# Moving the logarithm parts and their matrix passes within the woven order of a gated-linear-attention and squared-ReLU kernel

## The chip, the cores and the metric

The kernel runs on one core of one Trainium2 chip. The metric is the device time of one execution in microseconds, lower is better; the figure to start from is the median of eight runs. TensorE does the matrix products and the transposes, ScalarE (ACT) the logarithms, exponentials and many copies, VectorE (DVE) the elementwise work, SyncE (SP) issues all transfers between memory and the core.

## The reference

The first half is a recurrence over 768 time steps for 4 batches of 8 heads of 48 dimensions; the second half is a feed-forward layer with a squared ReLU on the 3072 rows that come out.

```python
def _attn_ref(q, k, v, alpha):
    B, H, S, D = q.shape                       # 4, 8, 768, 48
    state = np.zeros((B, H, D, D), dtype=np.float32)
    for t in range(S):
        state = alpha[:, :, t, :, None] * state + np.einsum('bhd,bhde->bhde', k[:, :, t], v[:, :, t])
        y[:, :, t] = np.einsum('bhd,bhde->bhe', q[:, :, t], state)

x = y.transpose(0, 2, 1, 3).reshape(B * S, H * D)     # 3072 x 384
h = np.maximum(x @ w_in, 0.0)                         # w_in 384 x 2048
out = (h * h) @ w_out                                 # w_out 2048 x 384
```

The kernel computes the recurrence in chunks: inside a chunk of 128 steps the running products of alpha are the exponentials of running sums of log(alpha). With b the running product, q is multiplied by b and k by 1/b, and the recurrence in a chunk becomes matrix products with a causal mask.

## The kernel before, in words

**Blocks, pairs and groups.** A block is one chunk of 128 steps of one batch, with all eight heads: 24 blocks, numbered `n`, four to a chunk position. Two blocks make a pair, four a group (`GB = 4`). The feed-forward layer works on one group of 512 rows at a time, six groups in all. While the layer works on group g, the attention of group g+1 is woven into its instructions.

**The attention of a block** is a row of small steps, named by functions: `ln` takes the logarithm of the block's alpha in place (ScalarE). `sp` splits it into two parts, `hi` rounded to the type fp32r and `lo` the rest (VectorE, lines 258 and 259). `cs` forms the running sums on TensorE: a triangular matrix times `hi`, then times `lo`, two passes that add up in one PSUM bank (lines 270 and 271). `eb` and `ei` are the exponentials of the sums and of their negatives (ScalarE, lines 278 and 282). `mq` and `mk` multiply q and k by them (VectorE, line 286). `bl` and `br` send the last row of b out to memory and back in another layout (SyncE). `turn` transposes q and k of both blocks (TensorE, line 535), `kc` and `qc` copy them out (ScalarE). `ga` and `gb` hold the scores, the masked copy, the chunk's state and the outputs `y`: bursts of 64 to 160 short matrix products on tiles of 48 or 64 rows (lines 400, 424, 450), with the mask, the sums and the next state on VectorE (lines 434, 461, 469, 470), and at the end of `gb` the copies of y into xT (ScalarE, line 558). The split exists from block 8 on (`SPLIT = 2 * GB`); the blocks before it multiply the unsplit logarithm.

**Buffers.** `hi` shares two buffers with the b of `eb` (tag "b"), `lo` two with the inverse of `ei` (tag "inv"). The sums of `cs`, the transposes, the scores and y all draw on one pool of four PSUM banks (`ps_att`); a bank is free again for a later tile, in program order, once the last reader of the tile in it is issued, and the first writer of the later tile waits for that reader. The product of a group's layer uses the other four banks.

**The layer from group 1 on** has two stages. First 38 us of `ffn_in_pair` (line 679) with no attention beside it. Its last steps are VectorE and ScalarE work on the hidden values (lines 692, 697, 698, 699) and one sum (line 590). Then 28 *units* of `ffn_product` (line 750), each eight matmul records of 128x192: four units to each of seven products, "1 5 6 7 2 4 3". After every unit of 5, 6 and 7 one sum on VectorE (line 590) prepares an operand of a later product.

**The order.** Nothing reorders this kernel: each engine's instructions run in the order in which the program lists them. The list is made by `weave`. A table, `PLAN`, gives each step a due time in units; a pair that starts at `t` has its step due at `t + at`. `weave` runs through the units and, ahead of unit u, issues every step whose due time is at most u, in order of due time, and those with equal times in order of the pairs. A digit behind a step's name says which block of the pair it is for. A `cs` step of block n also issues the load of block n+2's alpha, behind it in SyncE's queue; `ga`, `gb` and `turn` issue loads of k, v and q.

The pairs of split blocks and their starts: in group 1 blocks 8, 10 and 12 at t = 0, 7 and 14; in groups 2 and 3 blocks 14 and 18 at t = 0 and blocks 16 and 20 at t = 13.5; in group 4 block 22 at t = 0. Eight pairs in all. In group 0, whose layer is not of this form (units of `ffn_in` and `ffn_out`), blocks 4 and 6 are planned with due times stretched by 2.35, and the third pair there only closes block 6.

Of the kernel before, what the change touches and what calls it, by code (L numbers as in the profile page):

```python
# [24 lines left out]
def kernel(  # L25
# [224 lines left out]
    SPLIT = 2 * GB  # L250
# [564 lines left out]
    for word in first.split():  # L815
# [5 lines left out]


    PLAN = (
        (0, "ln0"),
        (0.5, "ln1 sp0"),
        (1.0, "sp1"),
        (2.0, "cs0 eb0 ei0"),
        (3.0, "cs1 eb1 ei1"),
        (3.5, "mk0"),
        (4.0, "bl0"),  # L830
        (4.5, "mq0 mk1 bl1"),
# [3 lines left out]
        (9.5, "ga"),  # L835
        (10.5, "gb"),
    )

    def attention(pairs, scale):


        out = []
        for t, n0, after, *last in pairs:
            for at, fs in PLAN:
                for f in fs.split():
                    w = t + at * scale
                    if f in ("ga", "gb"):
                        given = n0 - 2 if after else None, None if last or n0 >= NBLK else n0
                        out.append((w, {"ga": ga, "gb": gb}[f], given))
                    if last:  # L850
                        continue
                    if f == "ga" and n0 + 3 < NBLK:
                        out.append((w, load, (n0 + 3, "k")))
                    elif f == "gb":
                        for m, x in ((n0 + 2, "v"), (n0 + 3, "v"), (n0 + 4, "k")):
                            if m < NBLK:
                                out.append((w, load, (m, x)))
                    elif f == "turn":
                        if n0 < NBLK:
                            out.append((w, turn, (n0,)))  # L860
                            for m in range(n0 + 2, min(n0 + 4, NBLK)):
                                out.append((w, load, (m, "q")))
                    elif f != "ga" and n0 < NBLK:
                        n = n0 + int(f[-1])
                        out.append((w, steps[f[:-1]], (n,)))
                        if f[:-1] == "cs" and n + 2 < NBLK:
                            out.append((w, load, (n + 2, "a")))
        return sorted(out, key=lambda x: x[0])
# [18 lines left out]
    events += [(0, load, (GB + 1,)), (1.0, load, (GB + 2, "k"))]  # L887
    events += [(47 + 2 * r, sum_w_in, (r,)) for r in range(NR2 - 1)]
    events += attention([(0, GB, False), (18.0, GB + 2, True), (27.5, GB + 4, True, True)], 2.35)
    events += [(53, sum_x, (1,)), (54, sum_w_in, (NR2 - 1,))]  # L890
    weave(units, sorted(events, key=lambda x: x[0]))
    for g in range(1, NG):

        for j in range(NJ // 2 + 1):
            for i, step in enumerate("ABacCDd"):
                if j - step.islower() in range(NJ // 2):
                    ffn_in_pair(g, j - step.islower(), step)
                if g == 1 and j < NJ // 2 and i in (1, 4):
                    sum_w_out(2 * j + i // 4)
        events = []  # L900
        if g + 1 < NG:
            n = GB * (g + 1) + 2
            pairs = [(0, n, True), (13.5, n + 2, True)]
            if g == 1:
                pairs = [(0, n - 2, False), (7.0, n, True), (14.0, n + 2, True)]
            events = attention(pairs, 1) + [(NU - 3, sum_x, (g + 1,))]
        weave([(1, ffn_product, (g, *divmod(u, NR2))) for u in range(NU)], events)
# [30 lines left out]
```

## Time and profile before

| | |
|---|---|
| median of 8 runs | 568.5 us (568.05 to 571.26) |
| the profiled execution | 568.46 us, of which the span of the trace is 566.4 us |
| TensorE busy | 552.5 us, 98% of the span |
| weight loads | 470.1 us, 83% (they overlap the products) |
| VectorE / ScalarE busy | 339.9 us (60%) / 223.7 us (39%) |
| `cs` passes in the split blocks | 32: 16 on line 270, 16 on line 271 |
| `hi` / `lo` | 352 to 363 ns / 557 to 561 ns, 16 of each |

Matmul ends are modelled by the profile, so a busy TensorE is not TensorE at its peak. Where it loses time is read better from the distance between the starts of two neighbouring products than from the busy share. The stages lie as follows: group 1's `ffn_in_pair` ends at about 168.6 us and its units run to 225; then 38 us of `ffn_in_pair` and some 50 us of units for each of groups 2 (units 263 to 315), 3 (353 to 404) and 4 (442 to 488), and group 5 without attention to the end.

### The profile page before, as it was taken

Reading aid. Unit: us, or ns where it says so; the run is one execution under the profiler, and the core shown is the slowest. Engines: PE = TensorE matmul, PEld = TensorE weight load, DVE = VectorE, ACT = ScalarE, POOL = GpSimd, SP = SyncE. Lnnn points to the kernel's source line nnn. Section 1 sums busy time; section 2 is a strip of 40 time slices with the busy share of each in tenths; the row PEclk is TensorE's granted clock in tenths of the full one; section 3 lists DMA queues with packets and bytes.
Section 4 is the critical chain, followed back from the end, with each engine's and each line's share of the span. In section 5 each row is a group of like instructions: output and inputs, shape, how many; then the busy total and the mean of one; then the engine's idle time right before and its main releaser. Section 6 shows DMA issues by size and latency. Waiting matters only on the chain.

```text
span 566.4 us, 12584 instructions
## 1 busy us (share of the span) xinstructions
PE 552.5 (98%) x5306; PEld 470.1 (83%) x5306; DVE 339.9 (60%) x687; ACT 223.7 (39%) x533; POOL 5.9 (1%) x26
## 2 busy tenths in 40 slices
PE   8889999999999999999899999999999999999997
PEld 5754455668888999888899988999988999988996
DVE  4988688685875854566572566572466651466430
ACT  4469865442334353234243333432333340333100
POOL 2010000000000000000000000000000000000000
PEclk9999999999999999999999999999999999999999
DMA  9978577401003655000333200333300000100001
GB/s 164 253 175 219 144 163 238 114 1 57 1 1 56 114 97 104 30 1 17 55 72 77 65 2 0 57 72 58 86 0 1 0 3 1 57 0 1 1 0 57
DMA packets 117087, 37.04 MB, mean 65 GB/s; under 512 B 108820, under 2 KB 111912, under 8 KB 117032
## 3 DMA queue, kind: packets, MB, share of 16 engines
q1 hardware_dynamic: 117032, 36.25, 28.6%
q8 instruction: 42, 0.69, 0.5%
q14 instruction: 13, 0.11, 0.1%
HBM read 31.49 MB, written 4.75 MB: 64 GB/s over the span
## 4 chain that ended last, share of the span: by engine, by line
PE 62%; DVE 1%; ACT 1%; issue 1%
PE o L750 28%; PE h L679 27%; PE y L400 3%; PE sckv L424 1%; PE T L535 1%; PE sckv L450 1%; PE cs L271 1%; DVE lo L259 0%; ACT hid L698 0%; PE cs L270 0%; DVE hi L258 0%; DVE hid L692 0%; ACT hid L697 0%; DVE osb L784 0%; ACT qs L543 0%
## 5 line engine op out<-in xcount | busy, mean ns | idle before, releaser
L679 PE MATMUL h<-xT,w_in 128*128 128x256 f32 x480 | 124.0, 379 | 0.0
L679 PEld LDWEIGHTS h<-xT,w_in 128*128 128x128 f32 x480 | 91.1, 190 | 12.4
L750 PE MATMUL o<-w_out,hid 128*128 128x192 f32 x480 | 82.4, 326 | 0.0
L750 PEld LDWEIGHTS o<-w_out,hid 128*128 128x128 f32 x480 | 78.9, 190 | 0.4
L558 ACT COPY xT<-y 32x256 f32<-32x256 f32 (+2 forms) x132 | 46.2, 364 | 64.1 <-PE y L400 60.3
L692 DVE TENSOR_TENSOR hid<-h,u 128x256 f32<-128x256 f32 x120 | 50.8, 424 | 28.9 <-PE h L679 24.3
L697 ACT ACTIVATE hid<-hid 128x256 f32<-128x256 f32 x40 | 16.7, 417 | 114.6 <-DVE hid L692 114.6
L692 DVE TENSOR_TENSOR u<-h,u 128x256 f32<-128x256 f32 x80 | 33.9, 423 | 34.8 <-PE h L679 22.4
L679 PE MATMUL h<-s3x,ws 128*128 128x256 f32 x160 | 47.6, 379 | 0.0
L641 PE MATMUL h<-xT,w_in 128*128 128x512 f32 (+1 forms) x108 | 43.5, 550 | 3.3 <-ACT xT L558 1.8
L434 DVE COPY_PREDICATED am<-halves_mask,sckv 128x256 f32<-128x256 uint32 x40 | 15.6, 443 | 48.7 <-PE sckv L450 48.7
L716 PE MATMUL o<-w_out,hid 128*128 128x384 f32 x128 | 42.8, 490 | 0.0
L750 PE MATMUL o<-t,s 128*128 128x192 f32 x240 | 41.8, 327 | 0.0
L679 PE MATMUL h<-s3x,w_in 128*128 128x256 f32 x160 | 41.1, 379 | 0.0
L641 PEld LDWEIGHTS h<-xT,w_in 128*128 128x128 f32 x108 | 20.0, 190 | 23.4 <-issue 16.5
L750 PEld LDWEIGHTS o<-t,s 128*128 128x128 f32 x240 | 39.3, 190 | 0.2
L716 PEld LDWEIGHTS o<-w_out,hid 128*128 128x128 f32 x128 | 23.9, 190 | 16.2 <-issue 0.2
L679 PEld LDWEIGHTS h<-s3x,ws 128*128 128x128 f32 x160 | 30.4, 190 | 4.1
L679 PEld LDWEIGHTS h<-s3x,w_in 128*128 128x128 f32 x160 | 30.4, 190 | 4.1
L750 PE MATMUL o<-t,hid 128*128 128x192 f32 x160 | 28.1, 330 | 0.0
L784 DVE TENSOR_TENSOR osb<-o,us 128x384 f32<-128x384 f32 x10 | 5.6, 557 | 37.0 <-PE o L750 37.0
L699 DVE SCALAR_TENSOR_TENSOR hid<-hid 128x512 f32<-128x512 f32 x40 | 27.3, 682 | 0.0
(127 smaller groups left out, 767.9 us busy)
## 6 DMA issues: line engine op xcount, KB each, us to landing
raw<-in_moe_w_in_dram SPq DMA_DIRECT2D x8, 768.0 KB
raw<-in_moe_w_out_dram SPq DMA_DIRECT2D x8, 768.0 KB, 5.6
v_in<-in_v_dram SPq DMA_DIRECT2D x24, 192.0 KB, 3.8
out_dram<-osb SPq DMA_DIRECT2D x24, 192.0 KB, 2.1
k_in<-in_k_dram SPq DMA_DIRECT2D x23, 192.0 KB, 4.4
a_in<-in_alpha_dram SPq DMA_DIRECT2D x22, 192.0 KB, 3.6
q_in<-in_q_dram SPq DMA_DIRECT2D x22, 192.0 KB, 3.7
last<-row SPq DMA_DIRECT2D x40, 0.8 KB, 3.3
```

Source lines behind the costliest of these rows:

```text
L271: nc.tensor.matmul(out=out, lhsT=causal_r, rhs=lo, start=False, stop=True)
L400: ins = nc.tensor.matmul(out=ys[e][64 * half : 64 * half + D + G * e, m % 2, p // 2, t], lhsT=lhsT, rhs=rhs, start=(half, e) not in seen, ...
L424: nc.tensor.matmul(out=ps[e][HALF[h], 0, p, :], lhsT=ks[rows, p, HALF[h]], rhs=qs[rows, p, HALF[h]], start=True, stop=True, skip_group_che ...
L434: nc.vector.copy_predicated(out=am_h(n)[:, e, n % 2], data=ps[e][:, 0], mask=halves_mask.bitcast(U32).unsqueeze(1).to_broadcast([128, NP, ...
L558: copy(out=x[to : to + m, kk, t : t + 2], in_=blk[n]["y"][e][r : r + m, :, p // 2],)
L641: nc.tensor.matmul(out=ps, lhsT=w[:, kk, c0 : c0 + 128], rhs=xT[g][:, kk, cols], start=(kk == 0), stop=(kk == KM - 1),)
L679: nc.tensor.matmul(out=ps, lhsT=a, rhs=b, start=(step.isupper() and i == 0), stop=(i == len(pairs) - 1), skip_group_check=True,)
L692: nc.vector.tensor_tensor(out=o, in0=ps, in1=z, op=ALU.add)
L697: nc.scalar.activation(out=h1[:, HT : 2 * HT], in_=h1[:, HT : 2 * HT], func=AF.Relu)
L699: nc.vector.scalar_tensor_tensor(out=h2, in0=h2, scalar=0.0, in1=h2, op0=ALU.max, op1=ALU.mult)
L716: nc.tensor.matmul(out=acc[t][:, 0:DM], lhsT=hid[i][:, j, t * C : (t + 1) * C], rhs=w_out[i][:, j, :], start=(i == 0 and j == 0), stop=(i ...
L750: nc.tensor.matmul(out=acc[k][:, t, :], lhsT=lhs[:, j, t * C : (t + 1) * C], rhs=rhs[:, j, :], start=(first and r + j + t == 0), stop=(r = ...
```

## The change

`PLAN` gets new due times, and a second table, `EARLY`, keeps the old ones for blocks below 8, where there is no split.

```diff
     PLAN = (
-        (0, "ln0"),
-        (0.5, "ln1 sp0"),
-        (1.0, "sp1"),
-        (2.0, "cs0 eb0 ei0"),
-        (3.0, "cs1 eb1 ei1"),
+        (-1.0, "ln0"),
+        (-0.5, "ln1 sp0"),
+        (0.0, "sp1"),
+        (2.5, "cs0 cs1 eb0 ei0"),
+        (3.0, "eb1 ei1"),
         (3.5, "mk0"),
...
     )
+    EARLY = (
+        (0, "ln0"),
+        (0.5, "ln1"),
+        (2.0, "cs0 eb0 ei0"),
+        (3.0, "cs1 eb1 ei1"),
+    ) + tuple(x for x in PLAN if x[0] > 3)
...
-            for at, fs in PLAN:
+            for at, fs in EARLY if n0 < SPLIT else PLAN:
```

The logarithms of both blocks and their splits are due one unit sooner. The two passes of the second block come straight behind the two of the first: the first block's move half a unit later and the second's half a unit sooner. The exponentials of the first block move with its passes; those of the second keep their time. The loads of alpha that hang on `cs` move with them.

## The prediction

> **What bounds the kernel now.** The page first: TensorE is the busy engine all along, and its clock stays full.
>
> ```profile
> PE   8889999999999999999899999999999999999997
> DVE  4988688685875854566572566572466651466430
> PEclk9999999999999999999999999999999999999999
> ```
>
> TensorE is near nine tenths everywhere, VectorE at half, no slice below full clock. So only what holds TensorE up is worth anything, and a step moved on another engine matters only through TensorE. The table of waits names who holds it up near the change:
>
> ```profile
> PEld cs L271 <- DVE lo L259: 2.3, 6, 0.4
> PEld cs L270 <- DVE hi L258: 1.3, 4, 0.3
> PEld y L400 <- issue: 5.3, 13, 1.6
> ```
>
> Columns: total us, times, the longest. Weight loads of the logarithm passes wait 10 times, 3.6 us in all, for the parts hi and lo. Sixteen blocks have such passes, so not all wait. The timeline at the start of group 2's units:
>
> ```profile
> 263.10 2.76 PE L750 MATMUL o<-w_out,hid 128*128 128x192 f32 x16
> ...
> 265.86 0.56 DVE L259 TENSOR_TENSOR lo<-a_in,hi 128x384 fp32r<-128x384 f32 x1
> 265.88 0.19 PEld L270 LDWEIGHTS cs<-hi,causal_r 128*128 128x128 f32 x1 [0.32 <-DVE hi L258]
> ...
> 266.47 0.19 PEld L271 LDWEIGHTS cs<-lo,causal_r 128*128 128x128 f32 x1 [0.41 <-DVE lo L259]
> ...
> 266.73 0.56 DVE L259 TENSOR_TENSOR lo<-a_in,hi 128x384 fp32r<-128x384 f32 x1
> 266.75 1.46 PE L750 MATMUL o<-w_out,hid 128*128 128x192 f32 x8
> ...
> 268.05 0.19 PEld L271 LDWEIGHTS cs<-lo,causal_r 128*128 128x128 f32 x1
> ...
> 268.40 1.46 PE L750 MATMUL o<-w_out,hid 128*128 128x192 f32 x8
> ```
>
> Columns: start, duration, engine. Eight products take 1.46 us of which the last one's own 0.33 us overlaps what follows, so they step by (1.46 - 0.33)/7 = 0.162 us and a unit is 1.30 us. The last product of unit 1 starts at 263.10 + 2.76 - 0.33 = 265.53, the first of unit 2 at 266.75: 1.22 us for block 14's two passes. For block 15's two passes the same distance is 268.40 - (266.75 + 1.46 - 0.33) = 0.52 us, without a wait. The difference, 0.70 us, is TensorE standing still for the first block. The chain of waits runs through just this place (hidden values, hi, lo, pass), so it is on the path that sets the end.
>
> **The change part by part.** Due times are rounded up to whole units.
>
> *Pairs at t = 0 (blocks 8, 14, 18, 22).* Before: ln0 ahead of unit 0, ln1, sp0, sp1 ahead of unit 1, block 0's passes ahead of unit 2, block 1's ahead of unit 3. After: all logarithms and parts ahead of unit 0, all four passes ahead of unit 3. Units 0 to 3 put nothing on VectorE, and only unit 3 puts a copy on ScalarE, so the queues of both engines up to the parts are the same instructions in the same order: moving ln and sp is worth nothing here, because the parts are late through the sum on line 590 and the hidden values ahead of them, not through their place. What works is the later pass: unit 2 covers the wait. Four passes without a wait cost 2 x (0.52 - 0.16) = 0.72 us, as two separate pairs of them would. Gain 0.70 us a pair; starts in groups 1, 3 and 4 give the same 1.22 us (170.57 to 172.28, for instance), so 4 x 0.70 = 2.80 us.
>
> What is late next is the fourth pass. Unit 2 will start its last product at 263.10 + 23 x 0.162 = 266.83; the four weight loads then come about 0.00, 0.16, 0.34 and 0.51 us later (from 267.89 to 268.05 to 268.23 in this window for the first steps), the fourth at 267.34. The second lo ends at 266.73 + 0.56 = 267.29, and a load starts some 0.05 us after its part (265.86 + 0.56 = 266.42 against 266.47): 267.34. It is a dead heat. If it is lost, the wait itself is hundredths, and the restart costs about 0.1 us (266.47 to 266.75 is 0.28 us from pass to product, against 0.18 where nothing waited, 268.23 to 268.40). Between 0 and 0.15 us a pair; I take 0.03, 0.1 us in all, and keep 0.6 as the far end.
>
> The first block's exponentials now start some 0.6 us later. Behind them stands block 0's mk (267.86 now); its transposes start at 273.69, so 5 us cover it. Alpha loads behind the passes in SyncE's queue wait for lo, not for TensorE, and keep their times.
>
> *Pair at t = 7 (block 10).* The view by instruction of group 1:
>
> ```profile
> 183.24 0.41 PE L270 MATMUL cs<-hi,causal_r 128*128 128x384 f32 x1
> 183.74 0.44 PE L271 MATMUL cs<-lo,causal_r 128*128 128x384 f32 x1
> 184.02 1.46 PE L750 MATMUL o<-t,s 128*128 128x192 f32 x8
> 185.41 0.69 PE L424 MATMUL sckv<-qs,ks 48*64 48x64 f32 x32
> 185.92 0.65 PE L450 MATMUL sckv<-v_in,k_in 64*64 64x64 f32 x32
> 186.50 0.44 PE L270 MATMUL cs<-hi,causal_r 128*128 128x384 f32 x1
> ```
>
> The last product before the first pass starts at 182.92, the next at 184.02: 1.10 us, 0.58 more than the unhindered 0.52. The logarithms stand behind the copies ks and qs on ScalarE (182.09) and the parts behind line 590's sum of unit 7 (182.73). After: logarithms ahead of units 6 and 7, in front of those copies; the alpha they need was issued at 172.0 and 172.9 and lands a median 3.6 us later. The parts then fit VectorE's idle 1.95 us before 181.99 (hi and lo step by 0.38 and 0.47 us, four of them 1.8 us). The wait goes: 0.58 us.
>
> But the due times now tie: ga of block 8 (9.5) goes ahead of block 10's passes (9.5). The passes come behind ga's 64 products, where the second block's already were, and unit 10 follows. Which bank they get decides. If it were one that ga's scores just gave back, the passes would wait for VectorE's reads (mask from 186.62, states to 188.16): about 1.2 us for the first and 1.6 for the last. Before, block 11's pass had at 186.50 the choice of ga's two banks and two older ones and did not wait, although the mask was still to start: the bank longest free is taken. Two older ones, the transposes', are free after the change too. I take 0, and keep 1.6 us as the far end.
>
> SyncE's queue: alpha of block 12 (issued 183.76) now stands behind ga's load of k (186.66), which waits for the state products. It lands then at about 187.2 + 3.6 = 190.8; its logarithm is listed ahead of unit 13 (about 192) on a ScalarE that idles from 188.1 to 194.3, and the parts reach VectorE at about 195.7. Covered, with v and k loads half a microsecond later and 10 us ahead of use. If the cover failed, sums of later products on VectorE would queue behind that hi.
>
> *Pair at t = 14 (block 12).* Before, the first block waits again: the product at 196.68 + 1.14 - 0.33 = 197.49 is followed by one at 198.38, 0.89 us, 0.37 too many. After, the parts go between the sums of units 13 and 14 and are done near 197.5, using a VectorE gap of 0.78 us. The four passes stand behind ga (scores, states, 96 products of y) and do take the scores' banks, as y has the other two. VectorE's readers of them end at 202.07 and 202.60 when the scores end at 200.93; y takes 1.40 us and two passes 0.35, so the third pass comes at 202.68, just free. Bounds 0 to 0.3; I take 0.05. In gb, the scores of block 13 take the banks of these sums and so wait for four exponentials at a step of 0.39 us, about 1.6 us after the first; unit 17 and 32 products of y (1.30 + 0.62 us) cover that, with 0.4 to spare. Gain 0.37 - 0.05 = 0.32 us.
>
> *Pairs at t = 13.5 (blocks 16, 20).* Block 16's passes waited for nothing (0.51 us from product to product at 292.69). Parts: ScalarE is copying y until 289.79, so ln0 can't be sooner; VectorE takes hi at 290.37, lo, the sum of unit 13, hi, lo, in their steps of 0.39, 0.48, 0.60, 0.39 and 0.56 us: done at 292.8. The fourth pass, now ahead of unit 16 instead of 17, wants it at about 293.2. Gain 0, with 0.4 us of cover; without it 0.1 to 0.3 us a pair lost.
>
> *The sum.* 2.80 - 0.10 + 0.58 + 0.32 = 3.6 us, and perhaps 0.1 for fewer changes between passes and products (bounds 0 and 0.03 x 8 = 0.24). I take 3.7. From the profiled execution's own 568.46 (span 566.4, 2.06 around it): **564.8 us**. Its time is the median's to 0.04 us, so nothing is added. What TensorE starts moves with it, so I expect the gain to stay.
>
> A row that I can't place is the wait for "issue": TensorE waiting for nothing that the profile shows, in the midst of a burst of short products:
>
> ```profile
> 280.11 1.30 PE y L400 x82
> 281.41 1.51 issue
> 282.92 0.34 PE y L400 x7
> ```
>
> It comes once at this size, and 0.26 and 0.18 us at two more places of the chain. No burst is lengthened and only block 10's and 12's passes cross one, so it should stay: 0, with plus and minus 1.5 us as bounds.
>
> The Trainium skill, in "Runtime: NRT & Kernel Launch", section "Instruction fetch mechanics", says that an engine's instructions are brought in block by block and that crossing into the next block is mostly hidden. The 1.51 us in the rows above fits a block that came late better than a hidden one, though no row names it as that. By the page the sum stays at 564.8; by the row a shifted block may cost or save 1.5 us once.
>
> **Rivals.** (1) *Part of the gain goes into the next waits.* The dead heat at the fourth pass is lost four times (0.6 us) and the banks are given out the other way at t = 7 (1.6 us): 568.46 - 3.8 + 2.2 + 0.3 (block 12's bank) = 567.2 at worst, 566.2 with half of it. For it: margins of hundredths. Against: no wait for a bank at 186.50. (2) *No change that can be measured.* TensorE gains but finds VectorE late: in group 1 the transposes at 193.5 already follow the last mq closely (193.95 + 0.55 = 194.50, with q's transposes of the second block from 194.42). Then 568.0. Against: VectorE's work there is itself started by TensorE's units and scores, which move too, and it idles elsewhere. (3) *Slower, by the wait for issue.* The four passes stand closer to bursts in group 1 and every burst runs sooner against its instructions; if four of the bursts that follow get a stop of 1.51 us, the sum is -3.7 + 6.0 = +2.3: 570.8. It decides from three stops on (4.5 us). Against: only one of all bursts shows such a stop, and the bursts of groups 2 to 4 have the same instructions as before.
>
> **How the numbers follow.** A measurement of this kernel can tell about 0.2%, 1.1 us, from no change. Forecast 0.72 at 564.8, its own range 563.7 to 565.9; rival 1 0.13 at 566.2; rival 2 0.08 at 568.0; rival 3 0.07 at 570.8. The range reaches from a lucky 563.3 (the issue wait gone too) to 566.8, most of rival 1. Faster is the first two, 0.85; same 0.08; slower 0.07.
>
> **What would show it.** In the profile after: no waits of line 270 or 271 for hi or lo, or hundredths at the fourth pass; 0.87 to 0.9 us from unit 2's last product to unit 3's first in groups 1 to 4, and the passes of block 10 straight behind line 450 with no wait for lines 461 or 469. Units of groups 2 and 3 shorter by 0.7 us each, those of group 1 by about 1.6. Wrong would be: waits of line 424 for the exponentials, waits of line 271 above 0.2 us, new waits of the transposes for mq, or more "issue" in the chain.

## The result and the profile after

The changed kernel took 565.63 us (median of 11 runs, 564.63 to 566.9), the kernel before in the same comparison 568.89 us (32 runs). The ratio is 0.9942 with a 95% interval of 0.9932 to 0.9951: faster by 3.3 us, between 2.8 and 3.9, some 0.6%. The forecast was 564.8 us, 3.7 us less than before; the measured time lies in the forecast's own range of 563.7 to 565.9. The profiled execution took 565.49 us.

The page of the changed kernel, first lines:

```profile
span 563.4 us, 12588 instructions
...
PE 549.3 (98%) x5306; PEld 470.0 (83%) x5306; DVE 339.9 (60%) x687; ACT 223.2 (40%) x533; POOL 5.9 (1%) x26
```

The work is the same, yet TensorE is 3.2 us less "busy". In the units of groups 1 to 4 its busy time fell from 202.27 to 199.43 us while the units themselves became 3.79 us shorter: most of the waiting lay under records that count as busy. In the table of waits, no row of line 270 or 271 waiting for hi or lo is left. The timeline at the start of group 2's units (start, duration, engine):

```profile
262.32 4.06 PE L750 MATMUL o<-w_out,hid 128*128 128x192 f32 x24
...
265.09 0.56 DVE L259 TENSOR_TENSOR lo<-a_in,hi 128x384 fp32r<-128x384 f32 x1
...
265.95 0.56 DVE L259 TENSOR_TENSOR lo<-a_in,hi 128x384 fp32r<-128x384 f32 x1
266.06 0.19 PEld L270 LDWEIGHTS cs<-hi,causal_r 128*128 128x128 f32 x1
...
266.22 0.19 PEld L271 LDWEIGHTS cs<-lo,causal_r 128*128 128x128 f32 x1
...
266.40 0.19 PEld L270 LDWEIGHTS cs<-hi,causal_r 128*128 128x128 f32 x1
...
266.57 0.19 PEld L271 LDWEIGHTS cs<-lo,causal_r 128*128 128x128 f32 x1
...
266.92 1.46 PE L750 MATMUL o<-w_out,hid 128*128 128x192 f32 x8
```

Three units now run without a break. The second lo ends at 265.95 + 0.56 = 266.51, and the fourth weight load starts at 266.57 with no idle time against its row. From unit 2's last product (262.32 + 4.06 - 0.33 = 266.05) to unit 3's first it is 0.87 us, the forecast 0.88.

The stages of units in groups 1 to 4, one window each (start and end, length, busy times of TensorE, its weight loads, VectorE, ScalarE and GpSimd, clock, share and rate of the transfers):

```profile
169.44:224.34 54.90, 54.67 (x974) 51.73 (x973) 35.25 (x78) 25.03 (x70) 0.00 (x0) 1.00 0.51 96
262.32:313.82 51.50, 49.85 (x809) 47.76 (x808) 28.01 (x60) 20.04 (x56) 0.00 (x0) 1.00 0.37 71
351.81:401.31 49.50, 49.50 (x777) 47.74 (x776) 26.26 (x56) 20.04 (x56) 0.00 (x0) 1.00 0.36 70
439.30:484.71 45.41, 45.41 (x614) 43.94 (x613) 18.93 (x38) 15.15 (x42) 0.00 (x0) 1.00 0.03 10
```

Before, the same four stages took 56.49, 52.12, 50.36 and 46.13 us. They are shorter by 1.59, 0.62, 0.86 and 0.72 us, 3.79 us together. The span fell by only 3.0 us, because the first unit of group 1 began at 169.44 instead of 168.62 us. Up to there both kernels list the same TensorE instructions. In the ten profiles of this study that point lies between 168.41 and 169.81 us, so single executions differ by more than 1 us there.

At t = 7, block 10's passes stand behind the scores, next to block 11's (TensorE alone, by instruction):

```profile
185.09 0.65 PE L450 MATMUL sckv<-v_in,k_in 64*64 64x64 f32 x32
185.67 0.44 PE L270 MATMUL cs<-hi,causal_r 128*128 128x384 f32 x1
185.95 0.34 PE L271 MATMUL cs<-lo,causal_r 128*128 128x384 f32 x1
186.13 0.34 PE L270 MATMUL cs<-hi,causal_r 128*128 128x384 f32 x1
186.30 0.34 PE L271 MATMUL cs<-lo,causal_r 128*128 128x384 f32 x1
186.48 1.46 PE L750 MATMUL o<-t,s 128*128 128x192 f32 x8
```

VectorE began to mask the scores only at 185.79, after the first pass had started, so the passes had banks that the scores did not hold.

### The profile page after: what moved, and what is told of

Same layout as the page of the kernel before. It is cut to its first block, busy times and chain, and to the rows that moved or that the text cites. A ratio compares the mean times of both kernels' runs of the same rounds, so it can differ in the third digit from the quotient of the medians.

```text
span 563.4 us, 12588 instructions
## 1 busy us (share of the span) xinstructions
PE 549.3 (98%) x5306; PEld 470.0 (83%) x5306; DVE 339.9 (60%) x687; ACT 223.2 (40%) x533; POOL 5.9 (1%) x26
## 4 chain that ended last, share of the span: by engine, by line
PE 93%; DMA 2%; DVE 2%; SPq 1%; issue 1%; ACT 0%
PE h L679 34%; PE o L750 33%; PE o L716 8%; PE h L641 7%; PE y L400 4%; PE T L535 2%; PE sckv L424 2%; PE sckv L450 2%; DMA raw<-in_moe_w_in_dram 1%; SPq L115 1%; DMA t<-in_alpha_dram 1%; PE cs L267 1%; PE cs L270 1%; PE cs L271 0%; DVE w_in L179 0%
```

## The experiments

Each was timed against the kernel before on the same chip, e1 to e4 together and e5 to e7 together; the changed kernel had its own comparison. So times are set beside each other by their ratio to before. The passes are compared by distance: from the start of the last product ahead of them to the start of the first behind them.

| kernel | units of groups 1, 2, 3, 4 (us) | sum | median (us) | ratio to before |
|---|---|---|---|---|
| before | 56.49, 52.12, 50.36, 46.13 | 205.10 | 568.04, 568.32 and 568.89 | 1 |
| changed | 54.90, 51.50, 49.50, 45.41 | 201.31 | 565.63 | 0.9942 (0.9932 to 0.9951) |
| e1 passes only | 54.56, 51.50, 49.36, 45.41 | 200.82 | 564.84 | 0.9930 (0.9908 to 0.9952) |
| e2 parts only | 55.34, 51.72, 50.11, 46.13 | 203.29 | 566.83 | 0.9970 (0.9956 to 0.9984) |
| e3 apart | 54.51, 51.72, 49.37, 45.40 | 201.02 | 564.87 | 0.9931 (0.9906 to 0.9955) |
| e4 no cover | 55.92, 52.66, 50.59, 46.64 | 205.80 | 569.71 | 1.0021 (1.0006 to 1.0035) |
| e5 more cover | 55.05, 51.02, 49.79, 45.41 | 201.27 | 564.58 | 0.9937 (0.9924 to 0.9951) |
| e7 late lo | 55.14, 51.66, 49.72, 45.71 | 202.24 | 565.84 | 0.9953 (0.9939 to 0.9966) |
| e6 shift by 64 | 57.06, 49.45, 51.09, 45.41 | 203.00 | 566.49 | 0.9971 (0.9960 to 0.9981) |
| e6 shift by 128 | 56.70, 49.75, 49.35, 45.52 | 201.32 | 565.09 | 0.9947 (0.9935 to 0.9960) |

The units are those of one profiled execution each. Distances repeat to about 0.01 us, and so does group 4 in five of the six kernels whose passes wait for nothing there (45.40 to 45.41 us; the sixth took 45.52). The bursts of short products in groups 1 to 3 hold stops that differ by up to half a microsecond between kernels with the same TensorE instructions (last experiment). So a small difference between two sums says little, and the distances decide.

### One half of the change at a time

**e1, only the passes:**

```diff
-        (-1.0, "ln0"),
-        (-0.5, "ln1 sp0"),
-        (0.0, "sp1"),
+        (0, "ln0"),
+        (0.5, "ln1 sp0"),
+        (1.0, "sp1"),
         (2.5, "cs0 cs1 eb0 ei0"),
```

> Only the passes move; logarithms and parts keep their old due times. TensorE's own order is that of the changed kernel. Theory (the later place of the passes gives the gain; where the parts are listed gives nothing at t = 0): groups 2, 3 and 4 as in the changed kernel (units of 51.5, 49.5 and 45.4 us in its profile), group 1 at most 0.5 us longer, because the parts of block 12 then hold up VectorE in front of block 10's mask; in all 565.6 to 566.1 us, ratio to before 0.994 to 0.995. Rival (taking the logarithms and parts sooner is what pays): the waits for hi and lo come back at t = 0, 568 us, ratio 0.998 or more.

The units took 0.5 us less than the changed kernel's, not more, and the time, 564.84 us, is below the 565.6 to 566.1 expected. Groups 2 and 4 agree to 0.01 us. No pass waits for hi or lo. The feared delay at t = 14 is there but small: the distance is 1.18 us against 0.97 in the changed kernel, because the state on line 469 frees its bank later:

```profile
PEld cs L270 <- DVE s L469: 0.2, 1, 0.2
```

It is more than made up elsewhere in group 1: a stop among the score products, at 219.49 us in the changed kernel and shown there as 0.23 us of idle time for "issue", is missing here. From the first product of that burst to the first product behind it took 1.63 us there and 1.07 us here. So once the passes come later, taking the logarithms and parts sooner is worth 0.21 us at t = 14 by the distances, nothing at the other pairs, and nothing that shows in the time.

**e2, only the logarithms and parts:**

```diff
-        (2.5, "cs0 cs1 eb0 ei0"),
-        (3.0, "eb1 ei1"),
+        (2.0, "cs0 eb0 ei0"),
+        (3.0, "cs1 eb1 ei1"),
```

> Only logarithms and parts move; the passes keep their old places. Theory: the wait of 0.70 us stays at each of the four pairs at t = 0 (units of groups 2, 3 and 4 as before the change: 52.1, 50.4 and 46.1 us) and goes at t = 7 and t = 14 of group 1 (about 0.9 us): ratio to before 0.998 to 0.999, some 568 us. Rival (the parts' place carries it): 565.6 us, ratio 0.994.

The waits that stay are those at t = 0, four for each part:

```profile
PEld cs L271 <- DVE lo L259: 1.6, 4, 0.4
...
PEld cs L270 <- DVE hi L258: 1.3, 4, 0.3
```

The distances at t = 0 are 1.22 us as before. Those of block 10 and 12 fell from 1.10 to 0.52 and from 0.88 to 0.51 us, 0.95 us together. The ratio, 0.9970, is a little below the 0.998 to 0.999 expected. The units gained 1.81 us, 0.86 us more than that. Some 0.6 us of it comes from smaller stops for "issue" in groups 1 and 2 (0.26, 1.51 and 0.18 us became 0.05, 0.96 and 0.32), and the rest lies in group 3, where one burst of output products took 0.71 us before (396.48 to 397.19 us) and 0.48 us here, though the two kernels list the same TensorE instructions. Each half removes the waits for the parts in group 1, the passes alone at the cost of the wait for the bank; only the later passes remove those at t = 0.

### The stretch, or the unit in front of it

**e3, the second block's passes one unit later, so no stretch of four at t = 0:**

```diff
+    AT0 = PLAN[:3] + (
+        (2.5, "cs0 eb0 ei0"),
+        (3.5, "cs1 eb1 ei1"),
+    ) + tuple(x for x in PLAN if x[0] > 3)
...
-            for at, fs in EARLY if n0 < SPLIT else PLAN:
+            for at, fs in EARLY if n0 < SPLIT else AT0 if t == 0 else PLAN:
```

> As the changed kernel, but for pairs at t = 0 the second block's two passes go ahead of unit 4, the first block's stay ahead of unit 3: no stretch of four, and both pairs of passes covered. Theory (the cover counts, not the stretch): within 0.3 us of the changed kernel, ratio to before 0.994, no wait for hi or lo. Rival (four passes in one stretch save something of their own, such as a change of number type in TensorE): slower than the changed kernel by more than 0.3 us, up to the whole 2.8 us of those pairs.

Two separate pairs of passes have distances of 0.51 us each. Less one product step of 0.162 us, that is 0.70 us for both. The stretch's 0.86 to 0.87 us less one step is 0.70 us as well. Four passes together save nothing over two and two. No pass waited for hi or lo, and the units' sum is 0.29 us from the changed kernel's.

**e4, the stretch ahead of unit 2:**

```diff
-        (2.5, "cs0 cs1 eb0 ei0"),
+        (2.0, "cs0 cs1 eb0 ei0"),
```

> All four passes together, but due at 2.0 instead of 2.5: at t = 0 ahead of unit 2, so that unit 2 no longer covers the parts. Theory: the fourth pass waits for the second lo, 1.2 us at each of the four pairs at t = 0, 4.9 us in all, and nothing changes at t = 7, 13.5 and 14 beyond 0.3 us: about 570.4 us, ratio to before 1.002 to 1.004. Rival (the stretch itself is what pays): about 565.6 us, ratio 0.994.

TensorE alone at the start of group 2's units in e4:

```profile
263.79 1.63 PE L750 MATMUL o<-w_out,hid 128*128 128x192 f32 x9
265.44 0.44 PE L270 MATMUL cs<-hi,causal_r 128*128 128x384 f32 x1
266.04 0.44 PE L271 MATMUL cs<-lo,causal_r 128*128 128x384 f32 x1
266.31 0.43 PE L270 MATMUL cs<-hi,causal_r 128*128 128x384 f32 x1
266.90 0.44 PE L271 MATMUL cs<-lo,causal_r 128*128 128x384 f32 x1 [0.15 <-DVE lo L259]
267.18 1.14 PE L750 MATMUL o<-w_out,hid 128*128 128x192 f32 x6
```

The passes wait for hi, lo and the second lo in turn: 2.08 to 2.09 us from product to product instead of 0.87, 1.22 us more at each of four pairs, as expected; the stages' sum is 4.5 us above the changed kernel's. The kernel is 0.06 to 0.35% slower than before although its stretch of four is whole. The gain is the cover of unit 2, not the stretch.

### How near the fourth pass is

**e5, one unit more of cover:** `AT0` holds `(3.5, "cs0 cs1 eb0 ei0")` and `(4.0, "eb1 ei1")`.

> As the changed kernel, but at t = 0 all four passes go ahead of unit 4 instead of unit 3, one unit of 1.30 us more between the second lo and the fourth pass. Theory (the fourth pass was just in time in the changed kernel): no further gain, units of groups 1 to 4 within 0.3 us of the changed kernel's in sum (201.3 us in its profile), ratio to before 0.993 to 0.994. Rival (the fourth pass still loses hundredths to a tenth at each pair): 0.3 to 0.6 us less.

The distances at t = 0 are 0.86 to 0.87 us in both kernels, and group 4's units 45.41 us. The fourth pass lost nothing in the changed kernel. That the sums of all units agree as well, 201.27 and 201.31 us, is partly chance: group 2 is 0.48 us shorter and group 3 0.29 us longer, by other stops inside the bursts.

**e7, the second block's hi copied twice:**

```diff
         nc.vector.tensor_copy(out=hi, in_=la)
+        if n in (9, 15, 19, 23):
+            nc.vector.tensor_copy(out=hi, in_=la)
```

> As the changed kernel, but the copy to hi is done twice for blocks 9, 15, 19 and 23, the second blocks of the pairs at t = 0: one more copy of 0.38 us on VectorE ahead of the second lo. Theory (no slack at the fourth pass): it then waits about 0.4 us and restarts 0.1 us late at each of the four pairs, 1.9 us in all: about 566.9 us, units of each group some 0.45 us longer. Rival (unit 2 leaves slack): no change beyond 0.3 us.

The timeline of e7 at group 2, where line numbers are two higher from here on:

```profile
264.88 0.56 DVE L261 TENSOR_TENSOR lo<-a_in,hi 128x384 fp32r<-128x384 f32 x1
...
265.85 0.19 PEld L272 LDWEIGHTS cs<-hi,causal_r 128*128 128x128 f32 x1
...
266.14 0.56 DVE L261 TENSOR_TENSOR lo<-a_in,hi 128x384 fp32r<-128x384 f32 x1
...
266.22 0.19 PEld L272 LDWEIGHTS cs<-hi,causal_r 128*128 128x128 f32 x1
...
266.75 0.19 PEld L273 LDWEIGHTS cs<-lo,causal_r 128*128 128x128 f32 x1 [0.34 <-DVE lo L261]
...
266.86 0.85 PEld L752 LDWEIGHTS o<-w_out,hid 128*128 128x128 f32 x5
...
267.04 0.81 PE L752 MATMUL o<-w_out,hid 128*128 128x192 f32 x4
```

The copy made lo 0.40 us later (1.26 us behind the first lo instead of 0.86). Without a wait the fourth load would have stood 0.51 us behind the first (265.85 in this trace, so 266.36); it came 0.39 us later. So the slack in the changed kernel is about 0.01 us. The distance grew to 1.18 to 1.19 us at all four pairs, 0.32 us each, 1.28 us together. The expected 1.9 us was too much because I added 0.1 us for a restart, and there is none: the load behind the late one follows it after 0.11 us (266.86) instead of 0.18, which gives 0.07 us back. The units' sum grew by 0.93 us only, since the stops inside the bursts were smaller in this execution (group 2's is 1.20 us instead of 1.42); group 4, which has none, grew by 0.30 us.

### The stop for "issue"

The chain of waits of the changed kernel still holds the stop that I could not place:

```profile
278.62 1.28 PE y L400 x79
279.90 1.42 issue
281.32 0.35 PE y L400 x8
```

In its trace the queue that carries instructions moved one packet of 16 KB (16,384 bytes) from 278.35 to 279.59 us; the products go on 1.7 us after its end. Before the change: a packet from 279.94 to 281.37, products on at 282.92, 1.5 us later. The traces of the other runs show the same: every such stop of 0.9 us or more ends 1.4 to 1.8 us after the end of such a packet. To see whether this is code that comes late, I moved everything behind block 8's scores down TensorE's stream.

```diff
-        for p in range(NP):
+        for p in list(range(NP)) * (2 if n == 8 else 1):
```

> As the changed kernel, but the 16 score products of block 8 in group 1 are done twice (the same values again), 32 matmul records and 32 weight loads more, some 0.46 us, so that everything behind them stands 64 instructions later in TensorE's stream. Theory (the stop of 1.4 us for issue in group 2's ga, which ended 1.7 us after an instruction packet, is a block of instructions that comes late): it shrinks by at least 0.7 us or goes, and other stops may come at other bursts; units of group 2 near 50.1 us instead of 51.5. Rival (the stop has to do with the data or the work at that place): the same stop of 1.4 us at the same product.

> The same with the score products of block 8 done three times: 128 instructions later, some 0.93 us more in group 1. Theory: as for 64, the stop at group 2's ga changes or goes, units of group 2 near 50.1 us. Rival: the same stop at the same product, 51.5 us.

With 64 instructions more, the chain of waits has these stops of over 1 us behind group 1's start, in bursts that had none:

```profile
201.31 1.44 issue
...
369.23 1.51 issue
370.74 0.34 PE y L400 x6
```

Group 2 has none now and takes 49.45 us instead of 51.50; groups 1 and 3 have them. With 128 more, one of 1.17 us is left, at 218.08 us in group 1, and group 2 takes 49.75 us. That is less than the 50.1 us expected: by the starts of the products the stop in group 2 cost 1.63 us, more than its 1.42 us of idle time, and a small stop behind it went too. The work at each place was the same, so data and buffers do not explain whether a stop comes; its place in the stream does.

The packets moved with the inserted instructions: the last one ahead of group 2's units came 1.5 us ahead of them in the changed kernel (260.87 us), 8.6 us with 64 more (255.57) and 15.2 us with 128 more (249.26). How long the stop lasts is not set by the place. In the kernel before and in e2, which list the same TensorE instructions, the packet took 1.43 and 0.93 us and the stop 1.51 and 0.96 us. All this fits a block of instructions that comes late; no row names it as that, so this remains an inference. In all, shift 64 costs 1.7 us in the units, of which 0.47 us are its extra products, and shift 128 pays for its 0.93 us by fewer stops and ends where it began. Neither is better than the changed kernel. A shift that costs nothing was not tried.

## Why the prediction was right

**The place of the loss and its size.** The four waits at t = 0 were worth 0.70 us each by the distances 1.22 and 0.52 us. (For group 1 the forecast names 170.57 us, which is the start of a row of four products; the last of them starts at 170.57 + 0.81 - 0.33 = 171.05, and from there to 172.28 it is 1.23 us, the same to the rounding.) After, the four passes cost 0.70 us in place of 1.06 and 0.36, so 0.72 us a pair went. e1 and e4 show that the cover by unit 2 does this.

**"Moving ln and sp is worth nothing here."** Shown by e2 at t = 0, where nothing moved, and by e1. But the forecast credited the parts' new place with the 0.58 and 0.37 us at t = 7 and t = 14. e2 gives just these numbers. e1 shows that the later passes alone bring the 0.58 us as well, but at t = 14 only 0.15 us, as the wait for the bank takes 0.21. So the step was right in size; but the later passes do the work that it gives to the parts' new place, at t = 7 all of it and at t = 14 part of it.

**The dead heat** at the fourth pass was won four times, by about 0.01 us (e5, e7); the 0.1 us set aside for it was not spent. At this margin, which no row before the change could settle, that was luck, though little hung on it: by e7 a lo that came some hundredths later would have cost no more than those hundredths.

**Banks at t = 7** were given out as read from the pass at 186.50 in the profile before, at a cost of 0. At t = 14 the third pass did meet the bank: its weight load is at 201.46 and VectorE's reader ends at 200.98 + 0.42 = 201.40. The distance there is 0.97 us against 0.96 at t = 7, so it cost 0.01 us or so; 0.05 was taken.

**Blocks 16 and 20** gained and lost nothing: distances of 0.51 and 0.52 became one of 0.86 us, the same less the steps. The second lo ended at 290.64 + 0.56 = 291.20 and the fourth load was at 291.61, 0.4 us of cover as forecast.

**The sum.** The distances of all passes, less a step for each, fell by 3.8 us and the stages of units by 3.79 us, where 3.7 was forecast with 0.1 us kept for fewer changes between passes and products. e3 shows that this last term is 0; what balanced it is the allowance for the dead heat. The median shows 3.3 us, with an interval up to 3.9. In the profiled executions the rest lies in the stretch ahead of group 1, 0.82 us longer, a stretch whose length differs by more than 1 us between profiles with the same TensorE instructions. Whether the change has any part in that, and what the medians' difference consists of, was not settled.

**The rivals.** No new wait for a bank or a part cost more than hundredths. The forecast had named waits of line 424 for the exponentials as a sign of being wrong; one such wait of 0.23 us is there, at block 9's scores (187.87 us). Before the change there were two, and the same 0.23 us stands ahead of such bursts where only "issue" is named, so it is no loss from the change. VectorE was not the next limit. Rival 1 "with half of it" comes to 565.9 to 566.1 us by the forecast's own terms, not 566.2, at the edge of the forecast's own range. The wait for issue neither grew nor went: 1.42, 0.23 and 0.24 us, 1.9 us in all as before. e6 shows that stops can move, come and go as rival 3 feared, and that the place in the instruction stream decides it; this change only reorders TensorE's instructions and leaves their count ahead of group 2's burst all but the same. The Trainium skill, "Runtime: NRT & Kernel Launch", section "Instruction fetch mechanics", calls the crossing into a new block mostly hidden. Here 32 of the 42 packets come behind the start of group 1's units in the changed kernel, and behind 29 of them no burst stops for more than 0.1 us; but in every one of the ten traces one or two stops of 0.96 to 1.62 us inside a burst follow such a packet, and the measurement decides.

## What to carry to other kernels

When an engine that sets the pace waits in the middle of its queue, look for independent work that it already has behind the wait and put that in front: one unit of 1.30 us moved ahead was worth 0.70 us four times, while preparing the operand "sooner" did nothing there, as the preparing engine's queue did not change. Measure such waits by the distance between neighbouring products, since most of a wait can lie under records that count as busy (here 2.8 of 3.8 us). When a move gains, take the cover away again: that told the cover from the grouping, which looked like one edit.

## What was not expected of the hardware

Stops of TensorE inside bursts of short products, of 0.96 to 1.62 us, follow the place in the instruction stream: 64 instructions inserted in group 1 removed the one in group 2 and made two others, 1.44 us in group 1 and 1.51 us in group 3. Each ended 1.4 to 1.8 us after a packet of the queue that carries instructions.
